# Transposing the inner rows of half tiles: folding high and low parts on TensorE, or on VectorE

## The chip, the cores and the metric

The kernel runs as one program on one core of a Trainium2 chip. The metric is the device time of an execution in microseconds (us). A core has TensorE (PE in the profile; its weight loads are PEld), VectorE (DVE), ScalarE (ACT), GpSimd (POOL) and SyncE (SP), each with its own queue of instructions, and 16 DMA engines.

## What is computed

Three stages follow each other: a clustered attention (16 heads of 768 tokens), a feed-forward layer with a learned negative slope, and a mixture of eight experts with a skip rule. The change lies in the third:

```python
skip_score = x @ w_skip                 # x: 1536 x 512
xc = x[skip_score > 0]
e_idx = argmax(xc @ w_gate)             # one of 8 experts per row
for e in range(8):
    h = maximum(xc[e_idx == e] @ w1[e], 0.0)      # 512 -> 1024
    y[e_idx == e] = gate_w * (h @ w2[e])          # 1024 -> 512
out[skip_score > 0] = xc + y
```

## The kernel before

All matmuls of the experts run in a rounded fp32 form. To keep fp32 accuracy every operand is kept as a high part (the rounded value) and a low part (what is left), and a product is the sum of high x high, high x low and low x high.

The rows that take an expert are gathered into tiles of up to 128 rows. The experts' work is a list of units (one expert's weights, used by one or two tiles): tiles 0 and 1 in unit 0, 2 in unit 1, 3 and 4 in unit 2, 5 in unit 3, 6 and 7 in unit 4, 8 in unit 5, 9 and 10 in unit 6, 11 and 12 in unit 7, 13 in unit 8, 14 and 15 in unit 9. Tiles 1, 2, 5, 8, 12 and 15 are half tiles of 64 rows. A half tile puts its 64 high parts into columns 0 to 63 of the stationary operand and the 64 low parts into columns 64 to 127. Two products, with the weights' high and with their low part, then do the work of three (8 matmuls in place of 12 for 512 columns), but the result has two halves of 64 rows that must still be added.

A tile goes through these steps, for each of the two inner halves c of 512 values:

- `first(t, c)`: x times w1 into PSUM, then ScalarE moves the result into the SBUF tile `hb` (L1226; with the Relu for a full tile, without it for a half tile, whose halves aren't added yet).
- `transh(t, c)`: `hb` is turned by TensorE into a PSUM tile `pt`, ScalarE makes the high part `hTh`, VectorE the low part (`low()`: `hTl` on L1250, or, for a half tile, the second 64 columns of `hTh` on L1247).
- `second(t, c)`: `hTh` and `hTl` times w2, summed in PSUM over both c (L1197, as all matmuls of the stage).
- `output` and `scatter`: VectorE adds, GpSimd writes the rows by an indirect DMA (L1285).

In `transh` a half tile has its two halves added by TensorE on the way: the right-hand operand isn't the identity but `two`, 128 x 64, with ones at p and at p + 64:

```python
for k in range(4):
    nc.tensor.matmul(pt[:, k, :HALF], lhsT=r[:, k * P:(k + 1) * P], rhs=R["two"], start=True, stop=True)
nc.scalar.activation(a[:, :, :HALF], pt[:, :, :HALF], AF.Relu)
```

Weights come by DMA, issued by GpSimd (L1188), and each slice of 128 x 2048 is split by `ahead()`: ScalarE casts the high part (`hi`, L1453), VectorE subtracts for the low part (`lo`, L1457), called the conversion below. There are 40 slices, and five slots for converted ones; a slot is free again when its last product has run.

The order on every engine is the order in which the code is written. In the loop of `run` a turn is:

```python
if use and wsp.slots and n > 1:
    ahead()
first(t, c) if c < 2 else second(t, c - 2)
while wait:
    transh(*wait.pop(0))
```

so on ScalarE and VectorE the cast and conversion of a slice ahead stand in front of the `transh` of the half made one turn earlier. The copy and subtraction of the next tile's x (L1153, L1154; half tiles L1160, L1161) follow. At the start of the stage `begin` writes the same steps out by hand for tiles 0 to 4, mixed with the last steps of the routing. The buffers: three PSUM tiles for `pt`, two for `h`, two for `yo`; two SBUF tiles for `hb`.

Of the kernel before, what the change touches and what calls it, by code (L numbers as in the profile page):

```python
# [8 lines left out]
F32 = mybir.dt.float32  # L9
# [6 lines left out]
AF = mybir.ActivationFunctionType  # L16
ALU = mybir.AluOpType
AX = mybir.AxisListType
PSUM = bass.MemoryType.PSUM

P = 128
# [22 lines left out]
HALF = P // 2  # L44
# [1123 lines left out]
def moe2(ctx, tc, A, cst, R, y1d, wsp, wk, op, ps, x0, route, room):  # L1168
    nc = tc.nc
    ident = cst["ident"]  # L1170
# [36 lines left out]
    def is_half(t):  # L1207
        return TILES[t][2] < P
# [20 lines left out]
    def transh(t, c, late=None):  # L1229
        pt = ps["t"].tile([P, 4, P], F32, tag="t", name="pt")  # L1230
        r = hb.pop((t, c))
        a = wk.tile([P, 4, P], F32R, tag="hTh", name="hTh", bufs=HT)
        b = wk.tile([P, 4, P], F32R, tag="hTl", name="hTl", bufs=HT)
        hT[t, c] = (a, b)
        if is_half(t):

            for k in range(4):
                nc.tensor.matmul(pt[:, k, :HALF], lhsT=r[:, k * P:(k + 1) * P], rhs=R["two"], start=True, stop=True)
            nc.scalar.activation(a[:, :, :HALF], pt[:, :, :HALF], AF.Relu)
        else:  # L1240
            for k in range(4):
                nc.tensor.transpose(pt[:, k], r[:, k * P:(k + 1) * P], ident)
            nc.scalar.copy(a, pt)

        def low():
            if is_half(t):
                nc.vector.scalar_tensor_tensor(out=a[:, :, HALF:], in0=pt[:, :, :HALF], scalar=0.0, in1=a[:, :, :HALF].bitcast(F32),  # L1247
                                               op0=ALU.max, op1=ALU.subtract)
            else:
                nc.vector.tensor_tensor(out=b, in0=pt, in1=a.bitcast(F32), op=ALU.subtract)  # L1250
        if late is None:
            low()
        else:
            late.append(low)
# [33 lines left out]
    def begin():  # L1288
# [8 lines left out]
        next(route)  # L1297
        first(1, 0)
        transh(0, 0, low)
        first(0, 1)  # L1300
        transh(1, 0, low)
        first(1, 1)
        next(route)
        transh(0, 1, low)
        second(0, 0, (0,))
        gather(2)
# [154 lines left out]
def kernel(ctx, tc, A):  # L1461
    nc = tc.nc
# [4 lines left out]
    ident = cp.tile([P, P], F32, name="ident")  # L1467
# [20 lines left out]
    R = {}  # L1488
# [5 lines left out]
    def setup(sp):  # L1494
# [24 lines left out]
                                in1=i8.unsqueeze(1).unsqueeze(1).to_broadcast([P, 4, NE, NE]), op=ALU.is_gt)  # L1519
# [36 lines left out]
        R["e512"] = R["pool"].tile([P, NE], F32, name="e512")  # L1556
        nc.vector.tensor_scalar(out=R["e512"], in0=R["iota"][:, 1:NE + 1], scalar1=float(NPC * P), scalar2=None, op0=ALU.mult)
        yield
        two = R["two"] = R["pool"].tile([P, HALF], F32, name="two")
        nc.vector.tensor_tensor(out=two, in0=ident[:, :HALF], in1=ident[:, HALF:], op=ALU.add)  # L1560
        yield
        R["p0"] = R["pool"].tile([P, 1], F32, name="p0")
        nc.vector.tensor_scalar(out=R["p0"], in0=pf, scalar1=0.0, scalar2=None, op0=ALU.is_equal)
        yield
# [173 lines left out]
```

## Time and profile before

| | |
|---|---|
| median of 3 runs | 735.36 us (734.87 to 736.76) |
| the profiled execution's own time | 735.44 us |
| its span, first to last instruction | 733.5 us |
| TensorE busy | 707.3 us (96%) |
| VectorE busy | 566.0 us (77%) |
| ScalarE busy | 477.9 us (65%) |
| mean granted clock of TensorE | 0.993 of full speed |
| the twelve groups on L1238, matmuls | 12.0 us (96 instructions) |

Busy time is the sum of an engine's instruction durations. A wait is read from the timeline: the number in square brackets behind an instruction is how long its engine was idle before it, and what ended that. "x4" merges instructions that follow each other. A start-to-start distance, not a duration, says what a group costs on a busy engine, since instructions overlap at their ends. An fp32 matmul in the half tile's form shows as two loads and two matmuls.

### The profile page before, as it was taken

What the parts mean: (1) busy time and instruction counts of PE and PEld (TensorE: products, weight loads), DVE (VectorE), ACT (ScalarE), POOL (GpSimd) and SP (SyncE); (2) the same over time, 40 slices, a digit from 0 to 9 for tenths busy, and PEclk for the clock granted to TensorE, in tenths of its full rate; (3) what the DMA queues carried; (4) which work ended last, traced back from release to release, by engine and by line L of the source; (5) the groups of instructions that cost most, each with busy time, mean ns of one, the idle gap of its engine ahead of it and who ended that gap; (6) DMA issues with size and microseconds to landing.
All of it is one profiled execution on the core that took longest, in us unless ns stands there. A gap on an engine that the chain in (4) does not pass through costs nothing. (4 is left out here: it accounts for less than half of the span.)

```text
span 733.5 us, 11633 instructions
## 1 busy us (share of the span) xinstructions
PE 707.3 (96%) x4022; PEld 623.9 (85%) x4022; DVE 566.0 (77%) x1110; ACT 477.9 (65%) x916; POOL 375.0 (51%) x340
## 2 busy tenths in 40 slices
PE   9999999999999999999999999999999999999993
PEld 6988999889999899888889999998888778888872
DVE  5989888798989877888875989875478887775731
ACT  5878898788899955554446555656446676665620
POOL 4649778797796386666660000001127776583101
PEclk9999999999999999999999999999999999999997
DMA  7876668576656133333306200142618896867000
GB/s 210 226 170 170 125 134 198 146 176 128 172 144 155 52 110 126 116 115 115 115 0 210 93 2 0 58 109 111 241 44 314 313 404 247 321 226 304 18 10 25
DMA packets 46162, 109.22 MB, mean 149 GB/s; under 512 B 10779, under 2 KB 26587, under 8 KB 40721
## 3 DMA queue, kind: packets, MB, share of 16 engines
q1 hardware_dynamic: 39024, 67.81, 34.2%
q0 software_dynamic: 7072, 40.60, 14.7%
q8 instruction: 34, 0.56, 0.3%
q14 instruction: 32, 0.25, 0.1%
HBM read 74.78 MB, written 10.10 MB: 116 GB/s over the span
## 5 line engine op out<-in xcount | busy, mean ns | idle before, releaser
L341 DVE TENSOR_TENSOR etl<-pt,eth 128x384 fp32r<-128x384 f32 x192 | 102.2, 550 | 21.8 <-ACT eth L340 20.3
L340 ACT CAST eth<-pt 128x384 fp32r<-128x384 f32 x192 | 91.1, 486 | 20.4 <-PE pt L338 20.4
L338 PE MATMUL pt<-ident,e 128*128 128x128 f32 x576 | 93.7, 272 | 0.3 <-ACT e L327 0.3
L320 DVE TENSOR_REDUCE nm<-s 128x1 f32<-128x768 f32 x96 | 90.5, 943 | 3.2 <-PE s L307 2.9
L1165 POOL DMA_INDIRECT xg<-y1d,gi x16 | 26.3, 1646 | 130.1 <-DVE gi L1014 113.8
L327 ACT ACTIVATE e<-s,nm 128x768 f32<-128x768 f32 x96 | 87.5, 911 | 4.4 <-DVE nm L320 3.7
L695 ACT CAST gh<-gm 128x384 fp32r<-128x384 f32 x60 | 30.8, 514 | 82.0 <-DVE gm L693 58.5
L338 PEld LDWEIGHTS pt<-ident,e 128*128 128x128 f32 x576 | 73.6, 140 | 7.0 <-ACT e L327 0.5
L697 DVE TENSOR_TENSOR gl<-gm,gh 128x384 fp32r<-128x384 f32 x60 | 49.4, 823 | 25.7 <-ACT gh L695 25.1
L356 PE MATMUL px<-etl,vh 128*64 128x384 f32 (+1 forms) x192 | 65.7, 369 | 1.1 <-DVE etl L341 0.9
L304 PE MATMUL s<-AB 128*128 128x384 f32 x192 | 57.5, 380 | 2.3 <-ACT e L327 2.0
L667 PE MATMUL h<-xh,wh 128*128 128x384 f32 x256 | 55.8, 339 | 0.6 <-DVE gm L690 0.4
L667 PE MATMUL h<-xh,wl 128*128 128x384 f32 x256 | 56.0, 339 | 0.0
L567 POOL TENSOR_TENSOR pre<-ct,pre 128x512 int32<-128x512 int32 x26 | 37.2, 1453 | 35.9 <-DVE ct L565 35.9
L1285 POOL DMA_INDIRECT out_dram<-o,si x16 | 20.5, 1280 | 68.4 <-DVE o L1280 40.4
L667 PE MATMUL h<-xl,wh 128*128 128x384 f32 x256 | 55.0, 336 | 0.0
L358 PE MATMUL px<-eth,vh 128*128 128x384 f32 x160 | 53.9, 337 | 0.0
L1457 DVE TENSOR_TENSOR wl<-raw,wh 128x2048 fp32r<-128x2048 f32 (+2 forms) x26 | 44.3, 1712 | 11.6 <-ACT wh L1453 11.3
L307 PE MATMUL s<-CD 128*128 128x384 f32 x192 | 49.4, 338 | 1.0 <-DMA CD<-st 1.0
L667 PEld LDWEIGHTS h<-xh,wh 128*128 128x128 f32 x256 | 45.6, 188 | 3.3 <-DVE gm L690 0.5
L667 PEld LDWEIGHTS h<-xh,wl 128*128 128x128 f32 x256 | 44.6, 188 | 2.6 <-POOL wl L639 2.5
L667 PEld LDWEIGHTS h<-xl,wh 128*128 128x128 f32 x256 | 45.8, 188 | 0.0
(344 smaller groups left out, 1836.7 us busy)
## 6 DMA issues: line engine op xcount, KB each, us to landing
AB<-RL SPq DMA_DIRECT2D x32, 384.0 KB, 5.2
raw<-in_w_in_dram SPq DMA_DIRECT2D x16, 512.0 KB, 4.0
raw<-in_w_out_dram SPq DMA_DIRECT2D x16, 512.0 KB, 4.8
raw<-in_wall_dram SPq DMA_DIRECT2D x8, 1024.0 KB, 8.1
Tp<-in_qkT_dram SPq DMA_DIRECT2D x16, 384.0 KB, 3.7
CD<-RL SPq DMA_DIRECT2D x16, 384.0 KB, 6.5
raw<-in_wall_dram POOLq DMA_DIRECT2D x4, 1024.0 KB
vt<-in_v_dram SPq DMA_DIRECT2D x8, 384.0 KB, 6.1
```

The source lines that it names most:

```text
L304: nc.tensor.matmul(s[:, u, :384], lhsT=AB[:, 0, t * P:(t + 1) * P], rhs=AB[:, 1, ks], start=True, stop=False)
L307: nc.tensor.matmul(s[:, u, :384], lhsT=CD[:, 0, t * P:(t + 1) * P], rhs=CD[:, 1, ks], start=False, stop=True)
L320: nc.vector.tensor_reduce(out=nm, in_=s[:, :, :384], axis=AX.XY, op=ALU.max, negate=True)
L327: nc.scalar.activation(e.rearrange("p (u c) -> p u c", u=2), s[:, :, :384], AF.Exp, bias=nm, accum_out=den[:, i % 3:i % 3 + 1])
L338: nc.tensor.transpose(pt[:, i2], e[:, kt * P:(kt + 1) * P], ident)
L340: nc.scalar.copy(eh, pt)
L341: lows[u] = lambda: nc.vector.tensor_tensor(out=etl[:, 3 * u:3 * u + 3, q * P:(q + 1) * P], in0=pt, in1=eh.bitcast(F32), op=ALU.subtract)
L356: nc.tensor.matmul(px[:m], lhsT=vh[:, kt, :m], rhs=etl[:, kt], start=False, stop=False)
L358: nc.tensor.matmul(px, lhsT=vh[:, kt, :], rhs=eth[:, kt], start=False, stop=(kt == NT - 1))
L667: nc.tensor.matmul(hs[c], lhsT=a[:, k * P:(k + 1) * P], rhs=x[:, k, c * HC:(c + 1) * HC], start=(k == 0 and i == 0), stop=(k == KD - 1 and ...
L697: eng.tensor_tensor(out=gl[:, o], in0=m, in1=gh[:, o].bitcast(F32), op=ALU.subtract)
L1457: eng.tensor_tensor(out=lo[:, a:b], in0=self.src(t, c)[:, a:b], in1=hi[:, a:b].bitcast(F32), op=ALU.subtract)
```

## The change

For half tiles, `transh` uses the four ordinary transposes that full tiles use. `pt` then holds 128 columns for each of the four blocks, high parts in the first 64, low parts in the other 64. A new reduction on VectorE adds them (axis X is the innermost, here the two halves `s`), into `g`, which lies in the first 256 columns of `hb` itself. ScalarE's Relu and VectorE's low part read `g` in SBUF in place of `pt`. The constant `two` is gone.

```diff
+        for k in range(4):
+            nc.tensor.transpose(pt[:, k], r[:, k * P:(k + 1) * P], ident)
         if is_half(t):
-
-            for k in range(4):
-                nc.tensor.matmul(pt[:, k, :HALF], lhsT=r[:, k * P:(k + 1) * P], rhs=R["two"], start=True, stop=True)
-            nc.scalar.activation(a[:, :, :HALF], pt[:, :, :HALF], AF.Relu)
+            g = r[:, :4 * HALF].rearrange("p (k m) -> p k m", k=4)
+            nc.vector.tensor_reduce(out=g, in_=pt.rearrange("p k (s m) -> p k m s", s=2), axis=AX.X, op=ALU.add)
+            nc.scalar.activation(a[:, :, :HALF], g, AF.Relu)
         else:
-            for k in range(4):
-                nc.tensor.transpose(pt[:, k], r[:, k * P:(k + 1) * P], ident)
             nc.scalar.copy(a, pt)

         def low():
             if is_half(t):
-                nc.vector.scalar_tensor_tensor(out=a[:, :, HALF:], in0=pt[:, :, :HALF], scalar=0.0, in1=a[:, :, :HALF].bitcast(F32),
+                nc.vector.scalar_tensor_tensor(out=a[:, :, HALF:], in0=g, scalar=0.0, in1=a[:, :, :HALF].bitcast(F32),
                                                op0=ALU.max, op1=ALU.subtract)
...
-        two = R["two"] = R["pool"].tile([P, HALF], F32, name="two")
-        nc.vector.tensor_tensor(out=two, in0=ident[:, :HALF], in1=ident[:, HALF:], op=ALU.add)
-        yield
```

VectorE's row at tile 8 (unit 5), before. L1457 is a conversion (`wl`, `lastl`: low parts of a slice), L1154 the subtraction of the next tile's x, L1247 the half tile's low parts, L1250 those of tile 9:

```order
L1457 TENSOR_TENSOR lastl<-raw_3823,lasth 128x2048
L1154 TENSOR_TENSOR xTl<-pt,xTh 128x512
L1457 TENSOR_TENSOR wl_5969<-even_6291,wh_5968 128x2048
L1247 SCALAR_TENSOR_TENSOR hTh<-pt,hTh 128x4x64
L1154 TENSOR_TENSOR xTl<-pt,xTh 128x512
L1457 TENSOR_TENSOR wl_5614<-even_6542,wh_5613 128x2048
L1247 SCALAR_TENSOR_TENSOR hTh<-pt,hTh 128x4x64
L1250 TENSOR_TENSOR hTl<-pt,hTh 128x512
```

The same place after, with line numbers one lower:

```order
L1456 TENSOR_TENSOR lastl<-raw_3823,lasth 128x2048
L1154 TENSOR_TENSOR xTl<-pt,xTh 128x512
L1456 TENSOR_TENSOR wl_5967<-even_6289,wh_5966 128x2048
L1239 TENSOR_REDUCE hb<-pt 128x256
L1246 SCALAR_TENSOR_TENSOR hTh<-hb,hTh 128x4x64
L1154 TENSOR_TENSOR xTl<-pt,xTh 128x512
L1456 TENSOR_TENSOR wl_5615<-even_6540,wh_5614 128x2048
L1239 TENSOR_REDUCE hb<-pt 128x256
L1246 SCALAR_TENSOR_TENSOR hTh<-hb,hTh 128x4x64
L1249 TENSOR_TENSOR hTl<-pt,hTh 128x512
```

A reduction stands ahead of each half's low parts and behind the conversion that stood there already; tile 5 has the same pattern.

ScalarE's row at tile 8, after (before it reads `hTh<-pt` on L1239 where L1240 stands here, and is otherwise the same):

```order
L1226 ACTIVATE hb<-h 128x512
L1153 CAST xTh<-pt 128x512
L1452 CAST wh_5966<-even_6289 128x2048
L1226 ACTIVATE hb<-h 128x512
L1240 ACTIVATE hTh<-hb 128x4x64
L1153 CAST xTh<-pt 128x512
L1452 CAST wh_5614<-even_6540 128x2048
L1226 ACTIVATE hb<-h 128x512
L1240 ACTIVATE hTh<-hb 128x4x64
L1242 CAST hTh<-pt 128x512
```

No row has moved; the Relu reads what VectorE's reduction writes, and the copy of x and the cast of the next slice stand behind it.

## Rows read from the trace of the kernel before

**Rows 1.** Busy time by window: span, then each engine (instructions), clock, DMA, GB/s.
```profile
630.00:640.00 10.00, 10.00 (x57) 8.47 (x56) 8.65 (x7) 8.03 (x10) 3.70 (x2) 1.00 0.87 363
```

**Rows 2.** TensorE's waits from 555 us on: total, times, longest, in us.
```profile
PE pt L1242 <- ACT hb L1226: 1.6, 1, 1.6
PE yo L1197 <- DVE hTh L1247: 0.9, 1, 0.9
PE yo L1197 <- issue: 0.7, 1, 0.7
PE yo L1197 <- DVE hTl L1250: 0.3, 1, 0.3
```

**Rows 3.** One line's instructions, attention's reduction: ns min/median/max, first and last start.
```profile
L320 DVE TENSOR_REDUCE nm<-s x96: 915/947/959, 15.9 to 247.4; 128x1 f32<-128x768 f32 x96
```

**Rows 4.** Timeline at tile 5: start, duration, engine, line, operation, [idle before].
```profile
599.61 2.28 DVE L1457 TENSOR_TENSOR wl<-even,wh 128x2048 fp32r<-128x2048 f32 x1
...
599.84 0.39 ACT L1239 ACTIVATE hTh<-pt 128x256 fp32r<-128x256 f32 x1
...
600.57 1.93 ACT L1453 CAST wh<-even 128x2048 fp32r<-128x2048 f32 x1
...
602.46 1.09 PEld L1238 LDWEIGHTS pt<-two,hb 128*128 128x128 f32 x8
...
602.74 2.28 DVE L1457 TENSOR_TENSOR wl<-even,wh 128x2048 fp32r<-128x2048 f32 x1
...
603.47 0.77 PEld L1197 LDWEIGHTS yo<-lasth,hTh 128*128 128x128 f32 x4
...
604.94 0.41 DVE L1247 SCALAR_TENSOR_TENSOR hTh<-pt,hTh 128x256 fp32r<-128x256 f32 x1
...
605.22 0.59 PEld L1242 LDWEIGHTS pt<-ident,hb 128*128 128x128 f32 x4
...
605.78 0.77 PEld L1197 LDWEIGHTS yo<-wh,hTh 128*128 128x128 f32 x4
```

**Rows 5.** Timeline at tile 8.
```profile
634.06 2.29 DVE L1457 TENSOR_TENSOR wl<-even,wh 128x2048 fp32r<-128x2048 f32 x1
...
634.39 0.40 ACT L1239 ACTIVATE hTh<-pt 128x256 fp32r<-128x256 f32 x1
...
640.34 0.77 PEld L1197 LDWEIGHTS yo<-lasth,hTh 128*128 128x128 f32 x4
```

**Rows 6.** Timeline at tiles 1 to 4.
```profile
558.55 2.28 DVE L1457 TENSOR_TENSOR wl<-raw,wh 128x2048 fp32r<-128x2048 f32 x1
...
559.76 0.39 ACT L1239 ACTIVATE hTh<-pt 128x256 fp32r<-128x256 f32 x1 [0.18 <-PE pt L1238]
...
560.20 0.59 ACT L1153 CAST xTh<-pt 128x512 fp32r<-128x512 f32 x1
...
561.08 0.68 DVE L1154 TENSOR_TENSOR xTl<-pt,xTh 128x512 fp32r<-128x512 f32 x1
...
563.20 1.90 ACT L1453 CAST wh<-even 128x2048 fp32r<-128x2048 f32 x1
...
573.87 0.42 PEld L1242 LDWEIGHTS pt<-ident,hb 128*128 128x128 f32 x4 [1.98 <-ACT hb L1226]
```

**Rows 7.** Timeline at unit 4's first weight cast.
```profile
588.54 1.90 ACT L1453 CAST wh<-even 128x2048 fp32r<-128x2048 f32 x1 [6.56 <-DMA even<-in_wall_dram,wi]
```

**Rows 8.** Timeline at tiles 12 and 15.
```profile
680.48 0.42 DVE L1247 SCALAR_TENSOR_TENSOR hTh<-pt,hTh 128x256 fp32r<-128x256 f32 x1
...
683.61 0.89 PEld L1197 LDWEIGHTS yo<-wh,hTh 128*128 128x128 f32 x4
...
713.40 0.76 PEld L1197 LDWEIGHTS yo<-wh,hTh 128*128 128x128 f32 x4 [1.07 <-DVE hTh L1247]
```

**Rows 9.** Busy time by window at the end of the span.
```profile
720.00:722.00 2.00, 1.15 (x5) 0.57 (x4) 0.75 (x1) 0.00 (x0) 0.00 (x0) 1.00 0.02 6
...
726.00:728.00 2.00, 0.00 (x0) 0.00 (x0) 0.00 (x0) 0.00 (x0) 0.00 (x0) 0.50 0.02 4
```

## The prediction

> **What bounds the kernel now.** I read first the table of busy time in windows of 10 us over the expert stage, which runs from about 540 us to the end of the span. The change touches nothing that costs anything outside it. TensorE is busy for all 10 us of the window shown, at the full clock, while VectorE stands at 8.65 and ScalarE at 8.03 [rows 1]. Fifteen of the eighteen windows from 540 to 720 us say 10.00 for TensorE. Second, the list of waits on TensorE from 555 us on: four waits, 3.5 us in all [rows 2]. So TensorE is the bound. A microsecond taken from its own work is won only if nothing makes it wait instead, and a microsecond that it is made to wait is never got back, because it has no idle time later to take it from. What matters is therefore who feeds it, and how close. For that I read the timeline at the half tiles. There VectorE runs behind: at 599.61 it begins a 2.28 us conversion (the low parts of a weight slice, L1457), and only when this is done does it come to the half tile's low parts; ScalarE meanwhile had done the Relu at 599.84 and gone on to cast the next weight slice at 600.57 [rows 4]. Casting ahead while VectorE converts is what keeps the weights coming, and the margin is thin: the low parts of tile 5's second half are ready at 604.94 + 0.41 = 605.35, and TensorE begins the product that needs them at 605.78 [rows 4].
>
> **What is removed and added.** Twelve times (six half tiles, two inner halves each) TensorE's eight loads and matmuls on L1238 become the four of an ordinary transpose. At 602.46 the old form begins and the next product starts at 603.47: 1.01 us. At 605.22 a full tile's transposes begin and the next product starts at 605.78: 0.56 us [rows 4]. That is the same instruction with the same operands as in the new code, so each place gives TensorE back 0.45 us, twelve of them 5.4 us. VectorE gets twelve reductions that read 512 values out of PSUM and write 256. No such row exists. The reduction in the attention stage takes 947 ns for 768 values out of PSUM [rows 3]; VectorE's subtraction of 512 values out of PSUM takes 0.68 us [rows 6]; the low parts of 256 values take 0.41 us [rows 4]. I take 0.68 us, the row with the same number of values read, and keep 0.41 and 0.95 us as ends. The Relu and the low parts read SBUF in place of PSUM with the same 256 values; I leave them at 0.39 and 0.41 us. The constant that is no longer made is one small operation off the path: nothing. No DMA is added or removed.
>
> **What is moved.** The new wait is the point. ScalarE's Relu now waits for VectorE's reduction, and VectorE, which works in order, reaches that only after the conversion standing in front of it. Behind the Relu on ScalarE stands the cast of the next weight slice, and VectorE's next conversion waits for that cast. The two engines, which ran side by side, take turns. I go through the five places.
>
> Unit 3 (tile 5). The conversion begun at 599.61 ends at 601.89. The reduction ends at 602.57, so the Relu starts at 602.57 in place of 599.84, 2.73 us late [rows 4]. The cast follows the Relu by 0.73 us as now, at 603.30, and ends at 605.23 (1.93 us). The conversion, now at 602.74, starts there and ends at 607.51; then the second reduction, 608.19, Relu, 608.58, low parts, 608.99. TensorE's second product of tile 5 starts at 609.0 in place of 605.78: **+3.3 us**, with the two savings of 0.45 already inside the wait. Each reduction enters twice, so the ends are +2.7 and +3.8.
>
> Unit 5 (tile 8) has the same rows: conversion 634.06 to 636.35, reduction to 637.03, so the Relu is 2.64 us later than 634.39; cast by the same steps (0.73 and 1.93) to 639.69, conversion of 2.28 to 641.97, reduction, Relu, low parts to 643.45. The product now at 640.34 starts at 643.5 [rows 5]: **+3.2 us**, ends +2.6 and +3.7.
>
> Start of the stage (tiles 1 and 2). VectorE's conversion begun at 558.55 ends at 560.83; the Relu that ran at 559.76 without it now follows it. In a row: reduction 0.68, Relu 0.39, ScalarE's copy of tile 4 0.59, VectorE's subtraction 0.68, second reduction 0.68, Relu 0.39: 564.24, and only then the cast that starts at 563.20 now [rows 6]: 1.0 us late. ScalarE has hardly a gap from there to the row at 573.87, where TensorE already waits for it 1.98 us on the load side [rows 6], so the four savings of tiles 1 and 2 vanish in that wait and about 1 us is added. At 588.54 ScalarE waits 6.56 us for weights of unit 4 [rows 7]; their loads stand on GpSimd's queue behind the scatter of tile 1, which needs VectorE, so they may come later by as much, or not at all. I take **+1.0 us**, with ends -0.7 (the savings kept, waits hidden) and +1.5.
>
> Unit 7 (tile 12). The low parts of its second half come at 680.48, and TensorE needs them only at 683.61 [rows 8]. With a reduction, a Relu and themselves behind 680.48 they are done at 681.96, before 683.61 - 0.90. Both savings stay: **-0.9 us**, at worst -0.4.
>
> Unit 9 (tile 15). VectorE is not behind. TensorE waits 1.07 us for the low parts at 713.40 [rows 8]. Two savings bring the transposes 0.9 us forward, the reduction and its hand-over put 0.8 us back: **-0.1 us**, ends -0.4 and +0.2.
>
> The sum is 1.0 + 3.3 + 3.2 - 0.9 - 0.1 = +6.5 us. The profiled execution took 735.44 us (733.5 us of span and 1.9 us around it), 0.08 us above the median of the three runs. 735.44 + 6.5 = **741.9 us**.
>
> **The rivals.** (1) The savings arrive whole. It needs VectorE free whenever a half tile's transposes end, as at tile 15; then 735.44 - 5.4 = 730.0 us. Against it stand four rows in which VectorE is in the middle of a conversion when the Relu runs (558.55, 599.61, 634.06 against 559.76, 599.84, 634.39). This is the one on the other side; it decides where a conversion ends before the transposes do. (2) The reductions stand in VectorE's queue but ScalarE isn't held, because conversions start earlier and are out of the way at the first of the two halves. Then only the second half is late, at tiles 5 and 8: the conversion begun at 602.74 ends at 605.02 [rows 4], and 605.02 + 0.68 + 0.39 + 0.41 = 606.5 against 605.78, +0.7 each, with the start at -0.7: -0.7 + 1.4 - 1.0 = -0.3, 735.1 us. The order of ScalarE and VectorE, which is unchanged but for the reductions, speaks against it. (3) The clock of TensorE falls in the new waits. The granted clock is 1.00 (2.4 GHz) wherever I looked in this stage [rows 1] and 0.50 (1.2 GHz) at 726 us, where TensorE has had nothing to do since 721 us [rows 9]. The new waits at tiles 5 and 8 stand close together with short work between, and the trace before has no wait like them. If the eight matmuls behind each such wait ran at half clock, their 1.75 us (603.47 to 605.22) would double: 2 x 1.75 = 3.5 us more, 745.4 us. The Trainium skill (TensorE: Matmul & The Clock Gate, Part 4: PE-mode transpose) says that transposes do not count as TensorE activity the way matmuls do, which speaks for this one, since the change puts transposes next to the waits; no row here shows a drop beside a transpose.
>
> **How the numbers follow.** Forecast 0.72, (1) 0.07, (2) 0.11, (3) 0.10. About 0.3%, 2.2 us, is what a measurement of this kernel can tell from no change. Faster comes from (1), 0.07; same from (2), 0.11; slower from the forecast and (3), 0.82. The ends of the terms sum to -0.7 + 2.7 + 2.6 - 0.9 - 0.4 = +3.3 (738.7) and 1.5 + 3.8 + 3.7 - 0.4 + 0.2 = +8.8 (744.2); hand-overs between engines, which I left out of the chains, add a few tenths, and (3) lies at 745.4. The range is 738.7 to 745.5; (1) and (2) stay outside.
>
> **What would show it.** In the profile after: TensorE waits of roughly 2.5 to 3 us for the low parts ahead of the second product of tiles 5 and 8; ScalarE's Relu released by VectorE in nearly every case, about 2.7 us later against the transposes than now; the reduction at 0.6 to 0.8 us; no wait at tile 12, and at tile 15 one longer by about 0.7 us. TensorE's busy time should fall by about 5 us while the span grows. I am wrong if VectorE's conversions end before the transposes at tiles 5 and 8, if the reduction costs far from 0.68 us, or if ScalarE's casts turn out not to stand behind the Relu.

## The result, and the profile after

The changed kernel takes 745.5 us (median of 4 runs, 744.4 to 748.51), the kernel before 735.12 us beside it (4 runs, 734.7 to 736.76). The ratio is 1.0144, with an interval of 1.0117 to 1.0172: 10.6 us slower. The ratios here and below are those on record and differ a little from the quotient of the two medians. The profiled execution took 745.79 us, its span 743.9 us, against 735.44 and 733.5 us. The direction was right, and so were the places; the size was not. 745.5 us lies 3.6 us above the forecast, at the very end of the range.

TensorE's waits from 555 us on, the view of [rows 2] (in total, times, longest, us):

```profile
PE yo L1197 <- DVE hTh L1246: 9.7, 7, 2.7
PE pt L1236 <- ACT hb L1226: 1.9, 3, 1.6
PE yo L1197 <- ACT hTh L1242: 1.0, 1, 1.0
PE h L1197 <- DVE wl L1456: 0.6, 1, 0.6
PE yo L1197 <- DVE hTl L1249: 0.3, 1, 0.3
```

Four waits of 3.5 us have become thirteen of 13.5 us, and the first row, low parts of half tiles, holds 9.7 of them. The timeline at tile 5, which answers to [rows 4]:

```profile
602.97 2.28 DVE L1456 TENSOR_TENSOR wl<-even,wh 128x2048 fp32r<-128x2048 f32 x1
605.16 0.69 DVE L1239 TENSOR_REDUCE hb<-pt 128x256 f32<-128x512 f32 x1
605.94 0.42 ACT L1240 ACTIVATE hTh<-hb 128x256 fp32r<-128x256 f32 x1 [2.62 <-DVE hb L1239]
...
606.73 1.91 ACT L1452 CAST wh<-even 128x2048 fp32r<-128x2048 f32 x1
608.67 2.29 DVE L1456 TENSOR_TENSOR wl<-even,wh 128x2048 fp32r<-128x2048 f32 x1 [1.11 <-ACT wh L1452]
610.88 0.68 DVE L1239 TENSOR_REDUCE hb<-pt 128x256 f32<-128x512 f32 x1
611.60 0.42 ACT L1240 ACTIVATE hTh<-hb 128x256 fp32r<-128x256 f32 x1 [2.46 <-DVE hb L1239]
612.05 0.42 DVE L1246 SCALAR_TENSOR_TENSOR hTh<-hb,hTh 128x256 fp32r<-128x256 f32 x1 [0.48 <-ACT hTh L1240]
...
612.53 1.83 PE L1197 MATMUL yo<-wh,hTh 128*128 128x512 f32 x4 [2.69 <-DVE hTh L1246]
614.16 1.91 PE L1197 MATMUL yo<-wl,hTh 128*128 128x512 f32 x4
...
616.98 1.10 PE L1197 MATMUL h<-wl,xTh 128*128 128x512 f32 x4
...
651.92 1.20 PE L1197 MATMUL yo<-lasth,hTh 128*128 128x512 f32 x4 [2.68 <-DVE hTh L1246]
```

The rows up to 612.53 run in order of time: conversion, reduction, Relu, cast, conversion, reduction, Relu, low parts, product. VectorE and ScalarE take turns: the Relu waits 2.62 us for the reduction, and the second conversion waits 1.11 us for the cast that stands behind that Relu. Then see the rows at 612.53 and 614.16. Four matmuls take 1.83 and 1.91 us where a group takes 1.1 us. The reason is in the windows of 1 us (the stretch, its length, each engine's busy time with its instructions, and at the end granted clock, DMA share and GB/s); the last row is the same place at tile 8:

```profile
612.00:613.00 1.00, 0.47 (x2) 0.41 (x3) 0.90 (x2) 1.00 (x3) 0.70 (x2) 0.92 0.00 0
613.00:614.00 1.00, 1.00 (x4) 0.81 (x3) 0.21 (x1) 1.00 (x1) 0.78 (x1) 0.50 0.38 142
...
616.00:617.00 1.00, 1.00 (x6) 0.78 (x5) 0.61 (x1) 0.88 (x2) 1.00 (x1) 0.88 0.49 131
...
652.00:653.00 1.00, 1.00 (x5) 0.82 (x6) 0.60 (x1) 1.00 (x1) 0.73 (x1) 1.00 0.82 303
```

Behind the wait at tile 5 the granted clock is 0.50 (1.2 GHz) for some 3 us. Behind the wait of 2.68 us at tile 8 (651.92, the last row of the timeline) it stays at 1.00.

TensorE's starts at the same instructions in both timelines split the loss (us). The term is what the difference grows by from the landmark above.

| TensorE's row | before | after | difference | term | forecast |
|---|---|---|---|---|---|
| a matmul of the routing (L985) | 529.77 | 531.62 | +1.85 | +1.85 | 0 |
| tile 3, first half, transposes | 573.87 | 576.96 | +3.09 | +1.24 | +1.0 |
| tile 5, first half, transposes | 598.61 | 601.98 | +3.37 | +0.28 | in the +1.0 |
| tile 7, first half, transposes | 613.36 | 621.64 | +8.28 | +4.91 | +3.3 |
| tile 8, first half, transposes | 633.18 | 641.46 | +8.28 | 0 | 0 |
| tile 10, first half, transposes | 647.92 | 659.49 | +11.57 | +3.29 | +3.2 |
| tile 11, first half, transposes | 668.61 | 680.17 | +11.56 | 0 | 0 |
| tile 14, first half, transposes | 698.58 | 709.25 | +10.67 | -0.89 | -0.9 |
| end of the last matmul | 721.15 | 731.79 | +10.64 | -0.03 | -0.1 |

The same groups before:

```profile
605.80 1.18 PE L1197 MATMUL yo<-wh,hTh 128*128 128x512 f32 x4
...
608.69 1.09 PE L1197 MATMUL h<-wl,xTh 128*128 128x512 f32 x4
```

Of tile 5's 4.91 us, the slow clock is 1.56: from the first group behind the wait, at 612.53, to the fourth, at 616.98, pass 4.45 us, and before, from 605.80 to 608.69, 2.89 us. That leaves 3.35 us of waiting, with the two savings already in it. So two entries don't fit the forecast: 1.85 us ahead of the whole stage, and 1.56 us of clock. The experiments ask about both, and whether the queue is the cause of the rest.

### The profile page after: what moved, and what is told of

Its sections match the earlier page's. It is cut to its first block, busy times and chain, and to the rows that moved or that the text cites. A ratio compares the mean times of both kernels' runs of the same rounds, so it can differ in the third digit from the quotient of the medians.

```text
span 743.9 us, 11528 instructions
## 1 busy us (share of the span) xinstructions
PE 707.8 (95%) x3974; PEld 621.1 (83%) x3974; DVE 575.4 (77%) x1121; ACT 477.8 (64%) x916; POOL 366.5 (49%) x340
## 5 line engine op out<-in xcount | busy, mean ns | idle before, releaser
L1165 POOL DMA_INDIRECT xg<-y1d,gi x16 | 22.5, 1406 | 130.3 <-DVE gi L1014 113.8
L1284 POOL DMA_INDIRECT out_dram<-o,si x16 | 24.3, 1519 | 68.0 <-DVE o L1279 43.8
```

## The experiments

The forms are chosen tile by tile with this edit (the constant `two` is made as before); the tuple names the tiles that take the new form:

```diff
+        plain = not is_half(t) or t in (5,)
         for k in range(4):
-            nc.tensor.transpose(pt[:, k], r[:, k * P:(k + 1) * P], ident)
-        if is_half(t):
+            if plain:
+                nc.tensor.transpose(pt[:, k], r[:, k * P:(k + 1) * P], ident)
+            else:
+                nc.tensor.matmul(pt[:, k, :HALF], lhsT=r[:, k * P:(k + 1) * P], rhs=R["two"], start=True, stop=True)
+        g = pt[:, :, :HALF]
+        if is_half(t) and not plain:
+            nc.scalar.activation(a[:, :, :HALF], g, AF.Relu)
+        elif is_half(t):
```

**The 1.85 us ahead of the stage.** The changed kernel, with the three lines of `two` put back.

> The changed kernel with the constant `two` made again, though nothing reads it. Before 535 us, where no half tile exists yet, the changed kernel's profile is 1.85 us later than that of the kernel before; TensorE's granted clock falls to 0.50 at 20 to 24 us there, and to 0.65 at 8 to 12 us before. Theory, chance: when the clock falls there has nothing to do with the constant, so this takes about 745.5 us like the changed kernel, and either fall can be seen in its profile. Rival, the constant: without its operation VectorE's early steps move up and the fall lands on useful work; then with it this takes 745.5 - 1.85 = about 743.7 us, and its first 24 us look like those of the kernel before.

Measured: 744.7 us (742.32 to 748.6, 6 runs), ratio 1.0121 (1.0087 to 1.0154). By itself this lies between the two and settles nothing; the routing's matmul is at 530.74. And the rival was ill put: in the trace of the kernel before, the constant is made at 417.7 us, so nothing of it runs at 20 us.

```profile
L1560 DVE TENSOR_TENSOR two<-ident x1: 220/220/220, 417.7 to 417.7; 128x64 f32<-128x64 f32 x1
```

A later run tells more: the kernel before with a change of order in the expert stage alone (below), which has the constant and the old form. First the window of the kernel before, then that of this run, then that of the changed kernel:

```profile
20.00:24.00 4.00, 3.89 (x29) 3.52 (x29) 3.90 (x9) 3.05 (x8) 1.01 (x1) 1.00 0.97 225
```

```profile
20.00:24.00 4.00, 4.00 (x19) 3.98 (x18) 1.99 (x5) 1.69 (x4) 0.29 (x1) 0.50 0.97 211
```

```profile
20.00:24.00 4.00, 4.00 (x20) 4.00 (x19) 2.19 (x5) 1.85 (x4) 0.09 (x1) 0.50 1.02 213
```

The last two show the same fall of the clock on the same early work, and in this run the matmul of the routing is at 531.97. In the other traces, with the constant or without, that row lies anywhere from 528.88 to 531.77. The fall alone doesn't set it: with the three lines put back the clock never falls in the first 48 us, and the row is at 530.74. So nothing ties the 1.85 us to the change; they lie within what executions differ by, and from here on times are compared from this row on.

**Tile by tile.** Tiles 5, 8, both 12 and 15, and both 1 and 2 in the new form.

> Plain transposes and VectorE's sum at tile 5 alone; the other five half tiles keep the old form. Theory, VectorE's queue with the clock on top: the second product of tile 5 waits as in the changed kernel, +3.4 us, and the clock falls in that wait and costs 1.5 us more: 735.1 + 4.9 = 740.0 us, with a granted clock of about 0.8 at 605 to 615 us. Rival 1, the queue alone, the fall of the clock being a matter of chance or of what ran before: +3.4 us, 738.5 us, clock 1.00. Rival 2, tile 5 is late only because the start of the stage left VectorE late: under +1 us, at most 736.1 us.

Measured: 741.79 us (739.62 to 744.08, 6 runs), ratio 1.0086 (1.0055 to 1.0118). Behind the wait at tile 5:

```profile
607.61 2.08 PE L1197 MATMUL yo<-wh,hTh 128*128 128x512 f32 x4 [2.69 <-DVE hTh L1253]
609.49 1.91 PE L1197 MATMUL yo<-wl,hTh 128*128 128x512 f32 x4
611.20 1.91 PE L1197 MATMUL h<-wh,xTh 128*128 128x512 f32 x4
```

The same 2.69 us of wait with no other half tile changed: it isn't handed on from the start of the stage. Here the clock is at 0.50 for longer, from 607 to 613 us; between the same landmarks tile 5 costs 5.97 us. By the time, queue and clock together (4.9 us) lie in the interval of 4.0 to 8.7 us, and the queue alone (3.4 us) doesn't.

> Plain transposes and VectorE's sum at tile 8 alone. Theory, VectorE's queue: +3.3 us, 738.4 us, with one wait of about 2.7 us ahead of the second product of tile 8 and the granted clock at 1.00, as there in the changed kernel. Rival 1, the lateness is handed on from tiles 1, 2 and 5: under +1 us, at most 736.1 us. Rival 2, a wait of this length brings the clock down whenever it is the first of its kind: +4.8 us, 739.9 us, with a granted clock of about 0.8 around 645 to 655 us.

Measured: 741.26 us (740.23 to 742.84, 6 runs), ratio 1.0069 (1.0041 to 1.0096).

```profile
573.47 1.17 ACT L1283 COPY o<-yo 64x512 f32<-64x512 f32 x2 [2.58 <-DMA out_dram<-o,si]
...
577.12 0.66 PE L1238 MATMUL pt<-ident,hb 128*128 128x128 f32 x4 [3.83 <-ACT hb L1226]
...
578.97 1.91 PE L1197 MATMUL h<-wl,xTh 128*128 128x512 f32 x4
...
646.86 2.08 PE L1197 MATMUL yo<-lasth,hTh 128*128 128x512 f32 x4 [2.69 <-DVE hTh L1253]
```

Rival 2, by the trace (by the time, +5.1 us with an interval of 3.0 to 7.1, the theory's 3.3 is possible too): alone, the wait at tile 8 does bring the clock down, and tile 8 costs 4.56 us. In the run with the constant both falls are there. Of six waits of this kind in four traces five went with half clock behind them, for between 1.3 and 2.7 us of loss (what the place costs beyond the 3.29 us that it costs at the full clock, below); why the sixth, at tile 8 of the changed kernel, did not is left open. The first row above shows another thing: ScalarE waits 2.58 us for a scatter to leave its buffer, in code that is the same as before, where it waits 0.3 us. TensorE then waits 3.83 us for ScalarE ahead of tile 3, and behind that wait its clock is at half as well (0.50 from 579 to 581 us). The same is in four later traces whose tiles 1 and 2 have the old form: waits of 3.3 to 4.1 us at this place, half clock behind each, and 24.7 us from tile 3's transposes to tile 5's, where traces without it need as little as 23.2. The start of the stage swings by itself.

> Plain transposes and VectorE's sum at tiles 12 and 15 alone, where VectorE isn't behind. Theory: both savings of tile 12 arrive (-0.9 us) and tile 15 comes out even or a little better, -1.0 to -1.2 us: 734.0 us, faster than both kernels. Rival: TensorE's time isn't the limit there and the late waits take it back: 735.1 us; a reduction that holds up tile 15's low parts by its whole length would make it 735.5 us.

Measured: 733.87 us (732.34 to 736.64, 12 runs), ratio 0.9979 (0.9959 to 0.9998): 1.5 us faster, though the interval nearly touches 1. In the trace tile 12 gives 0.89 us and tile 15 0.03, as in the changed kernel. Where VectorE isn't behind, the change does what it says.

> Plain transposes and VectorE's sum at tiles 1 and 2 alone. Theory: the four savings vanish in the wait for tile 3's first half, and ScalarE's cast ahead of it comes later: +1.2 us, 736.3 us. Rival 1: the lateness is made up in ScalarE's wait for the weights of unit 4: no change, 735.1 us. Rival 2: the scatter of tile 1 and the weight loads behind it on GpSimd's queue come later too, +2.5 us, 737.6 us.

Measured: 735.58 us (734.36 to 737.43, 12 runs), ratio 1.0004 (0.9986 to 1.0022): no difference, as rival 1 has it, but the interval reaches to +1.6 us, and the theory's 1.2 is in it. Tile 3's transposes come 0.96 us later than before, counted from the routing's matmul, as expected. At tile 5 this trace is no longer behind that of the kernel before. ScalarE's wait for unit 4's weights, 6.56 us in [rows 7], is 2.99 us here:

```profile
586.54 1.90 ACT L1459 CAST wh<-even 128x2048 fp32r<-128x2048 f32 x1 [2.99 <-DMA even<-in_wall_dram,wi]
```

It is 2.59 us with tiles 12 and 15 alone, whose code up to here is that of the kernel before, and 6.81 us in the changed kernel. Where it is 6.56 us or more, TensorE then loses 1.6 to 1.8 us, where it is 5.59 us, 0.6, and in the other traces (4.81 us or less) TensorE doesn't wait behind it. The profile of before was one of the long ones: 1.6 us of its 733.5 were this. So rival 1's number came out, but not its reason: against the trace with tiles 12 and 15 alone, where the wait is short too, tile 5's transposes still come 1.02 us later (68.23 us behind the routing's matmul, against 67.21). What hides it is the swing. That distance is 67.05 to 71.39 us in the eight traces with the old form at tiles 1 and 2, and 68.08 to 70.36 in the six with the new.

**The order on VectorE.** The conversion, with the load that reuses its buffer, is issued behind a half tile's `transh`, not ahead of it.

```diff
             wsp.hi(n, c)
-            wsp.lo(n, c, nc.vector)
-            if n + 2 < n1:
-                loadw(n + 2, c)
+
+            def rest():
+                wsp.lo(n, c, nc.vector)
+                if n + 2 < n1:
+                    loadw(n + 2, c)
+            if wait and is_half(wait[0][0]) and (n, c) != now:
+                behind.append(rest)
+            else:
+                rest()
...
             while wait:
                 transh(*wait.pop(0))
+            while behind:
+                behind.pop(0)()
```

(`now` is the slice that the turn itself uses.) First on the changed kernel, then on the kernel before:

> The changed kernel with one more edit in the loop: where a half tile's `transh` follows in the same turn, the conversion (VectorE's low part of a slice ahead, and the load that reuses its buffer) is issued behind `transh` and not ahead of it. The same work, the reductions included; only VectorE's order differs, at tiles 5, 8 and 12. Theory, the queue: the reduction no longer stands behind 2.28 us, the two waits of 2.7 us and the fall of the clock go, tiles 5 and 8 cost 0 to 0.5 us each. The start of the stage, which this loop doesn't order, still costs about 1.2 us, tiles 12 and 15 give back about 1.1: 735.1 + 1.2 + 0.5 - 1.1 = 735.7 us, some 9 us less than the changed kernel. Rival, the work: twelve reductions more on VectorE cost the same wherever they stand, since VectorE sets the pace at the half tiles: at least 742 us.

Measured: 734.71 us (732.71 to 738.11, 12 runs), ratio 0.9985 (0.9966 to 1.0005). The timeline at tile 5:

```profile
600.83 0.68 DVE L1239 TENSOR_REDUCE hb<-pt 128x256 f32<-128x512 f32 x1
...
602.05 0.43 DVE L1246 SCALAR_TENSOR_TENSOR hTh<-hb,hTh 128x256 fp32r<-128x256 f32 x1 [0.55 <-ACT hTh L1240]
602.40 2.28 DVE L1465 TENSOR_TENSOR wl<-even,wh 128x2048 fp32r<-128x2048 f32 x1
...
604.60 0.68 DVE L1154 TENSOR_TENSOR xTl<-pt,xTh 128x512 fp32r<-128x512 f32 x1
605.20 0.68 DVE L1239 TENSOR_REDUCE hb<-pt 128x256 f32<-128x512 f32 x1
...
606.84 1.19 PE L1197 MATMUL yo<-wh,hTh 128*128 128x512 f32 x4 [0.42 <-DVE hTh L1246]
```

The same twelve reductions and the same instructions on all engines, and the loss of some 10 us is gone. Tile 5 costs -0.18 us between the landmarks, tile 8 -0.38, tile 12 -0.89, the start +1.34; the clock is 1.00 at tiles 5 and 8. This is the case against the work as such, and for the place in the queue.

> The kernel before (old form at all half tiles, TensorE adds) with the conversion behind `transh` as in the last run. It tells what the order alone is worth. Theory: in the old form ScalarE doesn't wait for VectorE, and the low parts have come before TensorE needs them, so nothing is won: 735.1 us, within 0.5 us. Rival: the order is better by itself (low parts 2 us earlier let TensorE start sooner) and gives 1 us or more, 734 us; or the conversions that come later make TensorE wait, 736 us and more.

Measured: ratio 1.0004 (0.9981 to 1.0028), median 736.73 us (733.25 to 740.09, 12 runs). No difference at tiles 5, 8 and 12 in the trace (0.02 us at most). The order alone is worth nothing that shows where ScalarE doesn't wait for VectorE.

**The clock.** Work that nobody reads fills the wait, ahead of the second product of tile 5:

```diff
     def second(t, c, which=range(3)):
         n = TILES[t][0]
+        if t == 5 and c == 1:
+            fill = ps["r"].tile([P, 4, P], F32, tag="r", name="fill")
+            for i in range(10):
+                nc.tensor.matmul(fill, lhsT=cst["identb"], rhs=cst["identb"].unsqueeze(1).to_broadcast([P, 4, P]), start=True, stop=True)
```

> Tile 5 alone in the new form, with ten matmuls of 128 x 512 bf16 ahead of its second product, about 2.2 us of work in the 2.7 us wait, whose results go to a PSUM tile that nothing reads. Theory: the clock falls because TensorE stands idle there; filled, it stays at 1.00, the eight matmuls behind the wait take 2 x 1.1 us in place of 2.08 + 1.91, and this takes about 1.5 us less than the kernel with tile 5 alone (741.8 us), 740.2 us. Rival: the fall comes from something else (the transposes next to the wait, which are there as before): the same slow matmuls, 741.8 us.

Measured: 739.68 us (738.29 to 742.3, 9 runs), ratio 1.0053 (1.0032 to 1.0075).

```profile
607.10 2.32 PE L1267 MATMUL fill<-identb 128*128 128x512 bf16 x10
609.96 1.20 PE L1197 MATMUL yo<-wh,hTh 128*128 128x512 f32 x4 [0.53 <-DVE hTh L1253]
610.99 1.10 PE L1197 MATMUL yo<-wl,hTh 128*128 128x512 f32 x4
```

The clock stays at 1.00, the groups take 1.2 and 1.1 us, and tile 5 costs 3.29 us between the landmarks: the forecast's 3.3, with nothing else in it. The time alone wouldn't decide: +3.9 us here and +6.3 with the wait empty have intervals that overlap.

> Tile 5 alone in the new form, as before with the wait filled, but with 20 transposes of the identity (fp32, 128 x 128, about 2 us) in place of the ten matmuls. Theory, any work does: TensorE is busy, the clock stays at 1.00, and this takes what the kernel filled with matmuls took, 739.7 us. Rival, by the Trainium skill (TensorE: Matmul & The Clock Gate, Part 4: PE-mode transpose), that transposes are not counted as matmuls are: the clock falls as in the empty wait, the matmuls behind it take about 2 us a group in place of 1.1, and this takes 741.8 us.

The filling is 20 times `nc.tensor.transpose(fill[:, i % 4], ident, ident)` in place of the ten matmuls. Measured: 739.2 us (736.77 to 742.86, 11 runs), ratio 1.0046 (1.0026 to 1.0066).

```profile
610.33 2.35 PE L1267 MATMUL fill<-ident 128*128 128x128 f32 x20
613.18 1.19 PE L1197 MATMUL yo<-wh,hTh 128*128 128x512 f32 x4 [0.50 <-DVE hTh L1253]
614.21 1.09 PE L1197 MATMUL yo<-wl,hTh 128*128 128x512 f32 x4
```

The clock is 1.00 in every window of 1 us from 605 to 617 us. The Trainium skill (TensorE: Matmul & The Clock Gate, Part 4: PE-mode transpose) says that a transpose doesn't count as work of the engine in the way a matmul does; here, for these 2.35 us of fp32 transposes, the rows show no such difference. It is the empty wait that goes with the fall.

> The changed kernel, all six half tiles in the new form, with the ten filling matmuls ahead of the second product of tile 5 and of tile 8. Theory: what the prediction left out is the clock; filled, the granted clock stays at 1.00 in both places and this is the prediction's own sum, 735.3 + 1.2 + 3.3 + 3.3 - 0.9 = 742.2 us, 2 to 4 us less than the changed kernel (745.5 and, with the constant, 744.7 us). Rival: the rest of the excess is something else that the change does elsewhere, and filling is worth under 1 us, at least 744 us.

Filled with the ten matmuls at tiles 5 and 8 of the changed kernel. Measured: 741.47 us (740.85 to 743.95, 6 runs), ratio 1.0081 (1.0057 to 1.0104), 6.0 us more than before. In both places:

```profile
608.96 1.20 PE L1197 MATMUL yo<-wh,hTh 128*128 128x512 f32 x4 [0.53 <-DVE hTh L1246]
...
646.84 1.20 PE L1197 MATMUL yo<-lasth,hTh 128*128 128x512 f32 x4 [0.52 <-DVE hTh L1246]
```

Between the landmarks tiles 5 and 8 cost 3.29 us each. With the clock held up, the changed kernel takes what the prediction said. That the clock fell not only in the profiled executions is seen in the mean granted clock that is on record for each: 0.986 on average over four of the changed kernel, 0.992 over the six filled ones, and 0.992 over the 28 of the kernel before beside them.

**A version faster than both?**

> All six half tiles in the new form, the conversion behind `transh` in the loop as in the earlier run, and now in the stage's opening too: the conversion of unit 1's last slice, and the load of unit 3's last slice that reuses its buffer, stand behind both of tile 2's `transh`. Theory, the queue: the opening no longer costs 1.2 us; ScalarE's cast for unit 2 comes about 0.5 us earlier than in the kernel before, so the start is -0.5 us (between -0.9 and 0), and with -0.2, -0.4 and -0.9 for tiles 5, 8 and 12 this is 735.3 - 2.0 = 733.3 us. Rival: TensorE then waits for the conversion that now comes late at tile 2's last product, or the late load holds up unit 3: 735 us and more.

```diff
-        wsp.lo(1, 3, nc.vector)
-        for c in range(1, NPC):
+        for c in range(1, NPC - 1):
             loadw(3, c)
...
         transh(2, 1)
+        wsp.lo(1, 3, nc.vector)
+        loadw(3, NPC - 1)
```

Measured: 735.0 us (733.9 to 737.3, 12 runs), ratio 0.9992 (0.9976 to 1.0007). ScalarE's cast for unit 2 does come 0.54 us earlier against the routing's matmul, but further on ScalarE waits for a scatter instead, and tile 3's transposes are 0.79 us late, not 0.5 us early:

```profile
564.04 1.89 ACT L1462 CAST wh<-even 128x2048 fp32r<-128x2048 f32 x1
...
572.39 1.18 ACT L1276 COPY o<-yo 64x512 f32<-64x512 f32 x2 [1.64 <-DMA out_dram<-o,si]
```

The 2.0 us that the theory promised are outside the interval; whether the late load or the swing of the start took them isn't shown.

> The new form at tiles 5, 8, 12 and 15 with the conversion behind `transh` in the loop; tiles 1 and 2 keep the old form. Theory: the start is as before, tiles 5, 8 and 12 give -0.2, -0.4 and -0.9: 735.3 - 1.5 = 733.8 us. Rival: the start made no difference anyway (tiles 1 and 2 alone in the new form took 735.6 us), and this is the same as the earlier run with all six in the new form, 734.7 us.

Measured: 734.54 us (731.49 to 737.07, 12 runs), ratio 0.998 (0.9962 to 0.9998), 1.5 us less than before, the theory's figure. It can't be told from the rival, since the run with all six in the new form (0.9985) differs by less than either interval. With tiles 12 and 15 alone it is the only version whose interval stays below 1, and both gain 0.2%, less than the 0.3% that I said a measurement can tell. So no version is shown to be clearly better than the kernel before.

## Where the prediction was right, and which step failed

- **The wait behind VectorE's queue: right.** ScalarE's Relu is released by VectorE in all twelve cases. At tile 5 it starts 3.96 us after the transposes (601.98 to 605.94) against 1.23 (598.61 to 599.84): 2.73 us later, the prediction's number. Tile 5's wait cost 3.35 us, and 3.29 with the clock held up (forecast 3.3, which by its own rows, 609.0 less 605.78, is 3.2); tile 8's 3.29 (3.2). The run with the conversion behind `transh` shows that the place in the queue is the cause.
- **The prices: nearly right.** The reduction takes 0.68 us. The Relu from SBUF takes 0.42 us where I left 0.39, and a hand-over from VectorE to ScalarE 0.1 us; together a few tenths for each chain.

```profile
L1239 DVE TENSOR_REDUCE hb<-pt x12: 682/685/692, 546.4 to 722.3; 128x256 f32<-128x512 f32 x12
L1240 ACT ACTIVATE hTh<-hb x12: 416/417/419, 547.1 to 723.1; 128x256 fp32r<-128x256 f32 x12
```

- **Tiles 12 and 15: right.** -0.89 and -0.03 us; no wait at tile 12, and at tile 15 a load waits 1.99 us where it was 1.07 in [rows 8].
- **The start: right in the trace, not to be told in the time.** +1.24 us to tile 3's transposes (forecast +1.0), and ScalarE's cast ahead of them is later by the same. But tiles 1 and 2 alone made no difference that can be measured, and one of 1.2 us isn't excluded either. ScalarE's waits for a scatter and for unit 4's weights, and the clock behind the first, move this stretch by up to 4.3 us from one execution to the next; that this one pair came out near the forecast is in part luck. I had read [rows 7] as slack of 6.56 us; it was one draw.
- **The clock: the step that failed.** The prediction put it into rival (3), at 0.10 and as two falls of 1.75 us, 3.5 together, and took it at zero in the sum; the forecast's reading was that TensorE goes on at 1.00 behind the new waits. The forecast itself asked for waits of 2.5 to 3 us; given those, a fall came in five of six, and it cost 1.3 to 2.7 us each time, 1.56 in the profiled execution. It belonged into the sum. The six waits lost 1.3, 1.3, 1.5, 1.6, 2.7 and 0 us, 1.4 on average; for tiles 5 and 8 that is 2.8 us more, +9.3 in place of +6.5, or 744.7 us. With the clock held up the kernel is 6.0 us slower than before (4.2 to 7.7), against the forecast's 6.5; with the waits empty 10.6, or 8.9 with the constant put back, so that filling them was worth some 3 to 4.6 us. Rival (3)'s 745.4 us is all but the measured time, but that is partly luck: the profiled execution has one fall and not two, and 1.85 us from ahead of the stage.
- **TensorE's busy time: wrong, only in part for the same reason.** It was to fall by 5 us; it is 707.8 us against 707.3. Some 1.7 us more of it lie ahead of the stage, where the clock fell at another place. From the routing's matmul on it is 186.6 us against 187.8, and tile 5's slow matmuls account for 1.56 of what is missing. The rest is open: between tile 8's landmarks, at the full clock, it fell by 0.11 us (14.63 against 14.74), where two savings are 0.9. The 48 records that are gone from it (3974 against 4022) show the shorter form.
- **The rest of the profiled difference** is the 1.85 us from ahead of the stage, within what traces of the same code differ by. The forecast had no error there, but a span taken from one profile carries about as much. Where the other three executions lost their time no trace shows.
- **Rivals (1) and (2) are out.** ScalarE was held at both halves of tiles 5 and 8, and the savings arrived only at tile 12. (Against rival (1) the prediction counts four rows; it names three places.)

## What to carry to other kernels

Before work is moved from the engine that sets the pace to one with idle time, look at what stands in that engine's queue at the moment the result is wanted: here a conversion of 2.28 us ahead of a reduction of 0.68 us cost 3.3 us twice, and the same reduction ahead of the conversion cost nothing. If a third engine has to wait for the result, everything queued behind its wait is late too. And where a forecast puts a wait of some microseconds on TensorE, price the matmuls behind it at half clock as well, in the sum and not as a rival: here ten of eleven waits of 2.7 to 4.1 us in the expert stage went with half clock.

## What the runs showed of the hardware that was not expected

After the same wait of 2.68 or 2.69 us TensorE's granted clock fell at different moments: before the wait was over (607 us with tile 5 alone, 0.50 in that row), just behind it (613 us in the changed kernel), about 1 us behind its end, or not at all.

```profile
607.00:608.00 1.00, 0.39 (x1) 0.39 (x2) 0.82 (x2) 1.00 (x3) 0.78 (x1) 0.50 0.00 0
```

```profile
652.00:653.00 1.00, 1.00 (x3) 0.77 (x3) 0.67 (x1) 0.29 (x1) 0.00 (x0) 0.50 1.02 434
```

(First row: tile 5 alone. Second: the changed kernel with the constant, at tile 8, where the product had begun at 650.53.) Loss by the clock is therefore a spread and not a constant, and a single profile shows one draw of it. In the one run that filled the wait with transposes, 2.35 us of them, the clock stayed at 1.00, as it did with 2.32 us of matmuls.
